# A recurrent-memory transformer block, forward and backward: two step loops whose x-attention was placed by a scheduler, written out engine by engine

## The chip, the cores and the metric

The kernel runs on one core of one Trainium2 chip. The metric is the device time of one execution in microseconds (us). Three executions of the kernel before took 8365.72, 8366.27 and 8371.87 us; the median is 8366.27 us.

## The reference

The input x has 2048 tokens of width 640. A layer norm gives xn. Branch A cuts xn into 64 segments of 32 tokens and carries a memory of 8 rows from one segment to the next, with 32 heads of 128 columns:

```
for s in range(64):
    h = concat([mem, xs])                     # 8 + 32 rows of 640
    q, k, v = h @ Wq, h @ Wk, h @ Wv          # each (32 heads, 40 rows, 128)
    scores = (q @ k.T) * scale
    scores = where(mask, scores, -1e9)        # memory rows see all 40, token rows look back
    o = (softmax(scores) @ v) @ Wo
    mem, out_s = o[:8], o[8:]                 # the new memory is the next step's input
```

Branch B is a gated feed-forward net (width 1728) on the same xn; the output is x + A(xn) * silu(B(xn)). The kernel also returns all gradients: of x, the first memory, Wq, Wk, Wv, Wo and the three matrices of B. Everything is bf16 with fp32 accumulation.

Only the eight memory rows make the 64 steps depend on each other. The 32 token rows of a segment need the memory as keys and values, but nothing waits for their outputs inside the loop.

## The kernel before

The work is done in phases, one after the other: layer norm and branch B forward; `phase3_Afwd`; `phase3b_out` (output projection); `phase4_Abwd`; `phase6_Awgrads` (weight gradients of A); `phase5_Bbwd_ln`.

`phase3_Afwd` first projects 672 tokens in one batch, and then runs the forward loop. `chain(t)` (L381) is the memory step: the projections of the new rows (L404, `packed_proj`, tile `pj`, 40 matmuls of 512 columns for each of v, k and q; 24 further tokens ride along in each step), the turned keys and queries (`packed_sel`), the scores of the memory rows (`psT`, L417), their softmax (L424 to L439), the product with v (`pom`, L448), the product with Wo (`packed_out`, L304, 64 matmuls of 320 columns), and `packed_fold` (L316), which turns the result into `hx`, the next step's input (L456).

The token rows are handled in tiles of three segments (`tl = t // 3`): 120 rows, in eight units of four heads. `kprep(tl, qd)` (L460) turns one unit's keys of the coming tile into `kT`; `xattn(tl, qd)` (L470) does one unit of the finished tile: load q and v, turn q (`qpt`), scores (`xsp`), maximum, exponentials on ACT (L501), normalising on POOL (`xP`, L506), turning (`xpp`, L510), product with v (`xpo`, L515), store. All turned tiles share one PSUM buffer (`tag="xt", bufs=1`), and most working tiles have one buffer.

The order on each engine is decided by the framework's scheduler: `chain(t)` is emitted under `tc.high_priority()` (L533), and the 16 units of a tile are emitted behind its three chain steps (L535). The first chain step of a tile reads all of the `kT` that eight `kprep` units have written.

`phase4_Abwd` is the same for the gradient, from the last step to the first: `chain(t)` (L639) with one projection (`packed_proj` of `gox`), `psd` (L682), the softmax gradient, `pgkv`, `pgq` (L721), three `packed_out` (L724) and `packed_fold` into `gox` (L729); `part1(tl, qd)` (L737) is a unit of the token rows. A tile's turned values are loaded at its first step as one tile `vTt` (L652), and the gradient rows go out to memory and come back in another layout (`gOst`, L670).

`phase6_Awgrads` (L835) goes over 8 groups of heads and, in each, 22 tiles: `t6` (L859) turns dS, three products `r6p` (L867), their turned copies `t6g` (L874), and 24 matmuls into the gradient of h (L882, L883).

SP (SyncE) issues most loads, POOL most stores, each in its own order; an issue that has to wait holds back those behind it.

Of the kernel before, what the change touches and what calls it, by code (L numbers as in the profile page):

```python
# [9 lines left out]
BF16 = mybir.dt.bfloat16  # L10
# [3 lines left out]
ALU = mybir.AluOpType  # L14
# [26 lines left out]
class K:  # L41
# [55 lines left out]
    def setup_consts(self):  # L97
# [17 lines left out]

        selb = const.tile([P, 2, 8], F32, name="selb")
        nc.gpsimd.memset(selb[:], 0.0)
        for a in range(2):
            nc.gpsimd.affine_select(out=selb[:], in_=selb[:], compare_op=ALU.not_equal, fill=1.0,
                                    base=-64 * a, pattern=[[-32, 2], [-1, 8]], channel_multiplier=1)  # L120
        self.selb = selb

    def build_masks(self, pool, scr):
# [21 lines left out]
        mcol = pool.tile([n, 3], F32, name="mcol")  # L145
        nc.vector.tensor_copy(mcol[:], a1[:, 0:nm].rearrange("p (s c) -> p s c", c=8)[:, :, 0])
# [10 lines left out]
        self.mask3, self.mask1, self.mcol = mask3, mask1, mcol  # L157

    def setup_dram(self):
# [18 lines left out]
        self.QS = mk("QS", (T, 32, HD))  # L178
        self.KS = mk("KS", (T, 32, HD))
        self.VS = mk("VS", (T, 32, HD))  # L180
        self.GOS = mk("GOS", (T, 32, HD))
        self.NB0 = 672
        self.QX0 = mk("QX0", (self.NB0, HD))
        self.KX0 = mk("KX0", (self.NB0, HD))
        self.VX0 = mk("VX0", (self.NB0, HD))
# [3 lines left out]
        self.PR, self.DSR, self.VTD = [], [], []  # L189
        for tl in range(self.NTL):  # L190
# [3 lines left out]
            self.VTD.append(mk(f"VTD{tl}", (P, H, n)))  # L194
        self.PM = mk("PM", (T, P, 240))
        self.GXP = mk("GXP", (T, P, 2, H, 8), F32)
# [13 lines left out]
    def x_src(self, tl, X0, XS, c0, c1):  # L210
        nx = self.geo(tl)[2]
        x0 = 96 * tl
        if x0 + nx <= self.NB0:
            return [(0, nx, X0[x0:x0 + nx, c0:c1])]
        t0 = (x0 - self.NB0) // 24
        if nx == 96:
            return [(0, 96, XS[t0:t0 + 4, 8:32, c0:c1])]
        return [(0, 24, XS[t0, 8:32, c0:c1]), (24, 32, XS[t0 + 1, 8:16, c0:c1])]
# [8 lines left out]
    def load_x(self, dst, off, srcs, eng):  # L227
        for (a, b, src) in srcs:
            eng.dma_start(dst[off + a:off + b, :], src)

    def load_m(self, dst, tl, XS, c0, c1, eng):
        ns, nm, nx, n = self.geo(tl)
        eng.dma_start(dst[0:nm, :], XS[3 * tl:3 * tl + ns, 0:8, c0:c1])
# [38 lines left out]
def packed_proj(k, ps, tag, x, W, st, cp):  # L272

    nc = k.nc
    for b in range(2):
        pj = ps.tile([P, 512], F32, name="pj", tag=tag)
        for dc in range(k.DC):
            for g in range(4):
                c0 = g * 1024 + b * 512
                nc.tensor.matmul(pj[32 * g:32 * g + 32, :], x[:, dc, :], W[:, dc, c0:c0 + 512],  # L280
                                 start=(dc == 0), stop=(dc == k.DC - 1), tile_position=(0, 32 * g),
                                 skip_group_check=True)
        k.copy(st[:, b * 512:(b + 1) * 512], pj[:], eng=cp[b])


def packed_sel(k, ps, tag, st):

    pk = ps.tile([P, 8, 4, 8], F32, name="psel", tag=tag)
    for j in range(8):
        k.nc.tensor.matmul(pk[:, j, :, :], st[:, j * P:(j + 1) * P], k.sel[:], start=True, stop=True)  # L290
    return pk


def packed_out(k, pm, srcs):

    nc = k.nc
    last = len(srcs) - 1
    for si, (x, W) in enumerate(srcs):
        for i in range(16):
            for a in range(2):  # L300
# [1065 lines left out]
```

## Time and profile before

| | |
|---|---|
| profiled execution, its own time | 8372.95 us |
| its span (first to last instruction) | 8371.2 us |
| TensorE matmul (PE) busy | 6051.0 us, 72% |
| TensorE weight load (PEld) busy | 3745.5 us, 45% |
| VectorE (DVE), ScalarE (ACT), GpSimd (POOL) busy | 29%, 20%, 14% |
| mean granted TensorE clock | 0.79 |

PE busy adds up the durations of matmuls that overlap in the pipeline, so it is no measure of how well the engine is used; the start of one matmul to the start of the next is. The granted clock is given as a share of 2.4 GHz: 1.0 is full speed, 0.5 is half (1.2 GHz). The rows that are used are in a section below.

### The profile page before, as it was taken

What the parts mean: (1) busy time and instruction counts of PE and PEld (TensorE: products, weight loads), DVE (VectorE), ACT (ScalarE), POOL (GpSimd) and SP (SyncE); (2) the same over time, 40 slices, a digit from 0 to 9 for tenths busy, and PEclk for the clock granted to TensorE, in tenths of its full rate; (3) what the DMA queues carried; (4) which work ended last, traced back from release to release, by engine and by line L of the source; (5) the groups of instructions that cost most, each with busy time, mean ns of one, the idle gap of its engine ahead of it and who ended that gap; (6) DMA issues with size and microseconds to landing.
All of it is one profiled execution on the core that took longest, in us unless ns stands there. A gap on an engine that the chain in (4) does not pass through costs nothing. (4 is left out here: it accounts for less than half of the span.)

```text
span 8371.2 us, 165393 instructions
## 1 busy us (share of the span) xinstructions
PE 6051.0 (72%) x67061; PEld 3745.5 (45%) x67142; DVE 2389.6 (29%) x7360; ACT 1672.1 (20%) x4414; POOL 1131.0 (14%) x1812
## 2 busy tenths in 40 slices
PE   7687666666666648576666777758888888787588
PEld 3354444444444435344444454545555555543234
DVE  5232222222222222233223233322222222202362
ACT  3232222222222221111111111111111111101111
POOL 0001111111111110233333333200000000000000
PEclk9796676666667769776666677789999999997699
DMA  5652222222222235433333344342222222246574
GB/s 186 219 172 66 77 78 75 75 71 76 74 77 74 82 95 155 144 108 107 107 105 111 106 119 122 100 98 72 71 70 71 71 74 78 74 104 170 175 193 103
DMA packets 858763, 880.27 MB, mean 105 GB/s; under 512 B 324472, under 2 KB 751944, under 8 KB 848272
## 3 DMA queue, kind: packets, MB, share of 16 engines
q1 hardware_dynamic: 507863, 542.29, 22.7%
q10 hardware_dynamic: 296440, 232.27, 9.5%
q0 software_dynamic: 53696, 95.13, 4.5%
q8 instruction: 529, 8.67, 0.5%
q14 instruction: 235, 1.92, 0.1%
HBM read 558.97 MB, written 310.36 MB: 104 GB/s over the span
## 5 line engine op out<-in xcount | busy, mean ns | idle before, releaser
L882 PE MATMUL g<-w,gT 128*96 128x512 bf16 (+1 forms) x2112 | 640.8, 401 | 0.0
L899 PE MATMUL wg<-gr,hr 120*128 120x512 bf16 (+1 forms) x2640 | 582.0, 379 | 5.2 <-DVE ghacc L888 3.6
L782 POOL DMA_DIRECT2D GXP<-gks x512 | 382.9, 861 | 711.8 <-DVE gks L90 637.4
L883 PE MATMUL g<-w,gT 128*96 128x128 bf16 (+1 forms) x2112 | 477.9, 226 | 0.0
L899 PEld LDWEIGHTS <-hr 120*128 120x128 bf16 (+1 forms) x2640 | 252.7, 98 | 322.8 <-issue 28.6
L92 ACT CAST gr<-r6p 120x512 bf16<-120x512 f32 (+1 forms) x352 | 205.8, 585 | 915.6 <-PE r6p L867 810.5
L510 PE MATMUL xpp<-ident,xP 120*120 120x120 bf16 (+1 forms) x704 | 109.3, 297 | 378.2 <-POOL xP L506 378.2
L882 PEld LDWEIGHTS <-gT 128*96 128x96 bf16 (+1 forms) x2112 | 271.6, 129 | 206.9 <-issue 41.7
L501 ACT ACTIVATE xE<-xsp,xnm 120x120 bf16<-120x120 f32 (+1 forms) x704 | 243.1, 356 | 380.9 <-DVE xnm L497 343.9
L304 PEld LDWEIGHTS <-gkv 128*8 128x8 bf16 x8192 | 226.2, 105 | 200.7 <-DVE gkv L715 39.0
L280 PEld LDWEIGHTS <-hx 128*32 128x32 bf16 x7680 | 206.8, 100 | 224.6 <-issue 49.3
L304 PE MATMUL gpm<-WvT,gkv 128*8 128x320 bf16 x4096 | 263.5, 444 | 32.8 <-DVE gkv L715 32.8
L506 POOL TENSOR_TENSOR xP<-xE,xrz 120x480 bf16<-120x480 bf16 (+1 forms) x176 | 168.9, 960 | 768.0 <-issue 428.9
L883 PEld LDWEIGHTS <-gT 128*96 128x96 bf16 (+1 forms) x2112 | 272.4, 129 | 0.0
L892 POOL CAST gxo<-ghacc 96x640 bf16<-96x640 f32 (+1 forms) x22 | 15.8, 716 | 1881.9 <-DVE ghacc L889 1842.6
L510 PEld LDWEIGHTS <-xP 120*120 120x120 bf16 (+1 forms) x704 | 77.0, 189 | 405.8 <-POOL xP L506 398.7
L304 PE MATMUL pm<-Wo,oTm 128*8 128x320 bf16 x4032 | 248.0, 430 | 4.2 <-DVE oTm L450 1.8
L682 PE MATMUL psd<-gmT,vTt 128*120 128x8 bf16 (+1 forms) x2048 | 150.8, 210 | 133.4 <-DMA vTt<-VTD 130.4
L888 DVE TENSOR_TENSOR ghacc<-ghacc,g 96x512 f32<-96x512 f32 (+1 forms) x154 | 105.2, 683 | 485.4 <-PE g L882 485.4
L515 PE MATMUL xpo<-vr,xPT 120*120 120x128 bf16 (+1 forms) x704 | 107.9, 293 | 162.2 <-DMA vr<-VS 77.5
L767 DVE CUSTOM_DVE_ANT_0 gprx<-gdp,gPx 96x120 f32<-96x120 f32 (+1 forms) x704 | 158.1, 270 | 233.8 <-PE gdp L762 209.2
L90 DVE CAST stg<-pj 128x512 bf16<-128x512 f32 x192 | 132.8, 692 | 314.5 <-PE pj L280 314.3
(298 smaller groups left out, 12032.5 us busy)
## 6 DMA issues: line engine op xcount, KB each, us to landing
OR<-xos POOLq DMA_DIRECT2D x168, 120.0 KB, 2.5
VTD<-gvT POOLq DMA_DIRECT2D x168, 120.0 KB, 3.6
vTt<-VTD SPq DMA_DIRECT2D x21, 960.0 KB
orr<-OR SPq DMA_DIRECT2D x8, 2520.0 KB
PR<-xP POOLq DMA_DIRECT2D x168, 112.5 KB, 3.4
dS<-DSR ACTq DMA_DIRECT2D x158, 112.5 KB
P<-PR SPq DMA_DIRECT2D x158, 112.5 KB
hb_tok<-HB ACTq DMA_DIRECT2D x40, 432.0 KB
```

What stands on the lines that cost most here:

```text
L92: return nc.scalar.copy(out, in_)
L280: nc.tensor.matmul(pj[32 * g:32 * g + 32, :], x[:, dc, :], W[:, dc, c0:c0 + 512], start=(dc == 0), stop=(dc == k.DC - 1), tile_position=(0 ...
L304: nc.tensor.matmul(pm[p0:p0 + 8, 0:320], x[:, h, :], W[:, h, 320 * b:320 * b + 320], start=(si == 0 and i == 0), stop=(si == last and i == ...
L501: nc.scalar.activation(E[0:n, j, :], sp[:, j, :], ACT.Exp, bias=nmx[0:n, j:j + 1], scale=k.scale, accum_out=Z[0:n, j:j + 1])
L506: nc.gpsimd.tensor_tensor(Pb[0:n], E[0:n], bc_last(rz[0:n], n), ALU.mult)
L510: nc.tensor.transpose(pp[:, j, :], Pb[0:n, j, :], k.ident[0:n, 0:n])
L682: nc.tensor.matmul(psd[:, h, :], vT[:, h, :], gmT[:, h, :], start=True, stop=True)
L767: nc.vector.tensor_tensor_reduce(pr[0:nx, j, :], dp[:, j, :], Px[0:nx, j, :], -k.scale, 0.0, ALU.mult, ALU.add, Dx[0:nx, j:j + 1])
L782: nc.gpsimd.dma_start(k.GXP[3 * tl + s, :, :, h0:h0 + 4, :], ks[:, s])
L882: nc.tensor.matmul(g5[0:nx, :], gT[:, i, j, 0:nx], Ws[i][:, j, 0:512], start=f, stop=l)
L883: nc.tensor.matmul(g1[0:nx, :], gT[:, i, j, 0:nx], Ws[i][:, j, 512:640], start=f, stop=l)
L899: nc.tensor.matmul(accs[dc][:], hr[0:n, tl, dc * P:(dc + 1) * P], grs[tl][0:n, i, :], start=(tl == 0), stop=(tl == NTL - 1))
```

## The change

Both loops are written in a fixed order. `in_order` ties each instruction of a loop to the one written before it on the same engine, so that the scheduler moves nothing. The x-attention unit is cut into stages (`turn_q`, `scores`, `soft`, `norm`, `turn_p`, `pv`; backward `turn`, `dprob`, `dsoft`, `gmem`), with loads of their own (`ld`, `ld_k`), and a table says which stage of which unit stands in which gap of the memory step (W0 to W2 between the projections, G1 to G6 between the later stages). Each step takes at most three units, but for the first backward step, which takes eleven; `pv` and the third `turn_p` of a unit come in the next step. In some gaps stand matmuls whose result nobody reads (`WARM`: 15 in a forward step, 10 in a backward step). The memory chain uses three fixed PSUM banks; the units rotate through five.

Other parts of the change: the memory rows look at their own segment's 40 rows rather than at the tile's 120; `vt`, `vTt` and `krow` hold one step rather than three; the fold sums its halves on ACT and DVE and turns a bf16 tile; `gOst` is turned on PE and no longer goes through memory; q and v share one DRAM tensor. In `phase6_Awgrads` the three products come in another order. Weight tiles of 96 or 120 columns are padded with zeros to 128.

```diff
+def in_order(k, start):
...
+    for ins in tc.nc.cur_bb.bb.instructions[start:]:
+        p = last.get(ins.engine)
+        if p is not None:
+            tc.add_manual_dep(ins, p.name, mybir.DependencyInfo(mybir.DependencyClass.NoSync, mybir.DependencyReason.DATA),
+                              reason="written order")
+        last[ins.engine] = ins
...
+def fold_add(k, pm, pool):
...
+    for c in (0, 160):
+        up = pool.tile([64, 160], F32, name="fup", tag="fup")
+        nc.scalar.copy(up[:], pm[64:128, c:c + 160])
+        nc.vector.tensor_tensor(fs[:, c:c + 160], pm[0:64, c:c + 160], up[:], ALU.add)
...
+            WARM = dict(G1=1, G2=2, G3=3, G4=4, G5=3, G6=2)
...
+                sk = stage()
+                half(Wk_, 0, sk, 'v')
+                half(Wk_, 1, sk, 'v')
+                gap("W0")
...
+                half(Wq, 1, sq, 'v')
+                gap("W1")
...
+                gap("W2")
+                psT = bview(bC, 40, 2, 8, 16)
+                for h in range(H):
+                    nc.tensor.matmul(psT[:, h // 16, :, h % 16], kT[:, h, 40 * s:40 * s + 40], qmT[:, h, :], start=True, stop=True)
...
+                gap("G1")
+                ps2 = bview(bC, P, 2, 40, bf=True)
...
+                gap("G2")
+                ps3 = bview(bC, 40, 2, P, bf=True)
...
+                gap("G3")
+                pom = bview(bC, P, H, 8)
...
+                gap("G4")
+                packed_out(k, pm, oTm, Wo, True, True)
+                fs = fold_add(k, pm, ch)
+                gap("G5")
+                pt = fold_turn(k, bC, fs)
...
+                gap("G6")
...
+                    for i in range(WARM.get(g, 0)):
+                        nc.tensor.matmul(bB[:], k.ident[:], Wq[:, 0, 0:512], start=True, stop=True)
...
+                if g == "W0":
+                    at(pv, t - 1, 0)
+                    at(turn_p, t - 1, 2)
...
+                elif g == "W1":
+                    at(pv, t - 1, 1)
+                elif g == "W2":
+                    at(pv, t - 1, 2)
...
+                elif g == "G1":
+                    at(scores, t, 0)
+                    at(turn_q, t, 2)
...
+                elif g == "G2":
+                    at(scores, t, 1)
+                    at(scores, t, 2)
+                    for u in kb[0:2]:
+                        kprep(*u)
...
+                elif g == "G3":
+                    at(soft, t, 0)
+                    at(soft, t, 1)
+                elif g == "G4":
+                    at(soft, t, 2)
+                    for i in range(3):
+                        at(norm, t, i)
+                elif g == "G5":
+                    at(turn_p, t, 0)
+                    at(turn_q, t + 1, 0)
...
+                elif g == "G6":
+                    at(turn_p, t, 1)
+                    at(turn_q, t + 1, 1)
+                    for u in kb[2:]:
+                        kprep(*u)
...
+            WARM = dict(G1=2, G2=3, G5=3, G6=2)
...
+                for a in range(2):
+                    nc.tensor.transpose(pgo[:, a, :], gmT[:, a].rearrange("p q h -> p (q h)"), k.ident[:])
+                nc.scalar.copy(gOst[:], pgo[:])
...
+                    if t == T - 1:
+                        if g == "G6":
+                            for u in batch[t]:
+                                ld_next()
+                                for f in (turn, dprob, dsoft, gmem):
+                                    f(*u)
...
+                    elif g == "W0":
+                        at(turn, t, 0)
+                    elif g == "W1":
+                        at(turn, t, 1)
+                        if t + 1 < T - 1:
+                            at(gmem_ld, t + 1, 2)
+                    elif g == "G1":
+                        at(dprob, t, 0)
+                    elif g == "G2":
+                        at(dsoft, t, 0)
+                    elif g == "G3":
+                        at(turn, t, 2)
+                        at(dprob, t, 1)
+                    elif g == "G4":
+                        at(dsoft, t, 1)
+                        at(gmem_ld, t, 0)
+                    elif g == "G5":
+                        at(dprob, t, 2)
+                        at(gmem_ld, t, 1)
...
-                for i, (lh, rh) in enumerate(((dST, kr), (dS, qr), (Pr, gor))):
+                for i, (lh, rh) in enumerate(((Pr, gor), (dS, qr), (dST, kr))):
```

On ACT in the forward loop, the stretch before the first step of a new tile read like this in the kernel before (`xE` are one unit's four exponentials, `qT` the copy of its turned queries, `xos` the copy of its result, `stg` a projection, `sTm` the memory scores):

```order
L92 CAST stg<-pj 128x512 x3
L92 CAST xos<-xpo 120x512
L486 COPY qT<-qpt 128x480
L501 ACTIVATE xE,xZ<-xsp,xnm 120x120 x4
L92 COPY kT_5752<-kpt 128x4x96
L486 COPY qT<-qpt 128x480
L501 ACTIVATE xE,xZ<-xsp,xnm 120x120 x4
L92 CAST xos<-xpo 120x512
...
L421 ACTIVATE sTm<-psT,mcol 120x256
```

One step of the changed kernel on ACT, from its `PTm` on (`xP` are now the exponentials, `fup` the fold, `xv` the result, `Em` the memory softmax):

```order
L604 ACTIVATE xP_5748,xZ<-xsp,xnm 120x120 x4
L604 ACTIVATE xP_5749,xZ<-xsp,xnm 120x120 x4
L604 ACTIVATE xP_5750,xZ<-xsp,xnm 120x120 x4
L348 COPY fup<-bank_5764 64x160 x2
L574 COPY xqT_5746<-qpt 128x4x120
L574 COPY xqT_5747<-qpt 128x4x120
L557 COPY kT_5741<-kpt 128x12x32
L634 CAST xv<-xpo 120x512 x2
L92 CAST stg<-bank_5764 128x512
L92 CAST stg<-bank_5765 128x512
L634 CAST xv<-xpo 120x512
L491 CAST sTm<-bank_5766 40x256
```

The exponentials of three units now stand together behind one another, and their results' copies stand in the next step; before, a unit's copies and exponentials alternated, one unit behind the other, between the projections and `sTm`.

On SP in the backward loop, the kernel before issued in this order around a tile's first step (`vTt` is the tile's 128x3840 load, `gOst` the gradient rows that come back, `gqx`, `gvr`, `gor`, `gPx` the loads of a unit):

```order
L668 DMA GOS<-gstg 4x32x1024
L652 DMA vTt<-VTD 128x3840
L670 DMA gOst<-GOS 128x1x128 x2
L229 DMA gqx<-QS 96x1x512
L233 DMA gvr<-VS 24x1x512
L229 DMA gvr<-VS 96x1x512
L229 DMA gor<-GOS 96x1x512
L663 DMA xp<-GXP 128x512
```

In the changed kernel (`gqv` is q and v of a unit together, `vTt` one step's 128x1280):

```order
L848 DMA xp<-GXP 128x8x64
L888 DMA GOS<-gstg 4x32x1024
L963 DMA gqv<-QVS 24x2x512
L246 DMA gqv<-QVS 96x2x512
L246 DMA gor_40752<-GOS 96x1x512
L970 DMA gPr<-PR 120x480
L832 DMA vTt<-VTD 128x1280
L834 DMA gPm<-PM 128x80
L837 DMA Qst<-QVS 128x1x128 x2
L842 DMA krow<-KS 8x4096
```

The `vTt` that is issued here belongs to the step after the one whose gradient rows `GOS` stores; before, it belonged to the same step and the `psd` of that step waited for it. `gOst` has left the queue.

## Rows read from the trace of the kernel before

**Rows 1.** Windows of four stretches: us, busy time by engine, granted clock, DMA share, GB/s.

```profile
core 0: us, PE busy (x) PEld busy (x) DVE busy (x) ACT busy (x) POOL busy (x), PEclk, DMA share, GB/s
599.00:2936.00 2337.00, 1578.11 (x21112) 988.20 (x21112) 605.11 (x1550) 613.88 (x2138) 392.02 (x587) 0.69 0.26 75
2936.00:3085.00 149.00, 50.33 (x415) 34.16 (x415) 31.77 (x96) 42.12 (x196) 36.29 (x59) 0.50 0.27 74
3421.00:5457.00 2036.00, 1395.10 (x24223) 957.38 (x24224) 626.46 (x3161) 314.26 (x779) 672.33 (x1107) 0.71 0.40 108
5540.00:7400.00 1860.00, 1554.46 (x11662) 949.84 (x11660) 474.25 (x1091) 300.33 (x588) 15.76 (x22) 0.97 0.24 71
```

**Rows 2.** Timeline of DVE, forward loop: start us, us; the end of three steps.

```profile
1442.07 0.20 DVE L456 CAST hx<-pfold 128x40 bf16<-128x40 f32 x1 [0.90 <-PE pfold L316]
1506.68 0.20 DVE L456 CAST hx<-pfold 128x40 bf16<-128x40 f32 x1 [1.15 <-PE pfold L316]
1530.76 0.20 DVE L456 CAST hx<-pfold 128x40 bf16<-128x40 f32 x1 [0.97 <-PE pfold L316]
```

**Rows 3.** Timeline inside the long step: one x-attention unit, and the next one's start.

```profile
1468.98 0.66 PE L492 MATMUL xsp<-kT,qT 128*120 128x120 bf16 x4 [0.70 <-ACT qT L486]
...
1472.54 0.98 POOL L506 TENSOR_TENSOR xP<-xE,xrz 120x480 bf16<-120x480 bf16 x1 [3.38 <-issue]
...
1477.45 0.66 PE L492 MATMUL xsp<-kT,qT 128*120 128x120 bf16 x4 [0.70 <-ACT qT L486]
```

**Rows 4.** Waits of PE, 1200 to 2600 us: total us, times, longest.

```profile
PE xpp L510 <- POOL xP L506: 186.5, 75, 4.2
```

**Rows 5.** Windows: a short step, part of a long one, two `packed_out` (columns as Rows 1).

```profile
1418.00:1442.00 24.00, 19.90 (x309) 12.30 (x306) 7.33 (x18) 6.37 (x20) 3.20 (x5) 0.79 0.32 91
...
1457.00:1504.00 47.00, 22.40 (x209) 15.58 (x213) 9.73 (x27) 12.46 (x50) 9.82 (x14) 0.50 0.25 73
1411.80:1415.90 4.10, 4.10 (x64) 2.04 (x64) 0.41 (x1) 0.00 (x0) 0.08 (x1) 0.54 0.29 95
4125.90:4130.40 4.50, 4.50 (x136) 2.87 (x128) 0.00 (x0) 0.00 (x0) 0.00 (x0) 1.00 0.20 62
```

**Rows 6.** Timeline of PE: one group of each kind at the full clock.

```profile
1410.28 0.99 PE L448 MATMUL pom<-PTm,vt 120*128 120x8 bf16 x32 [0.46 <-ACT PTm L445]
...
1418.25 2.34 PE L280 MATMUL pj<-Wv,hx 128*32 128x512 bf16 x40
...
1452.61 0.43 PE L515 MATMUL xpo<-vr,xPT 120*120 120x128 bf16 x4
...
1453.05 0.38 PE L490 MATMUL xsp<-mask,ident 120*120 120x480 bf16 x1
...
4125.96 2.34 PE L304 MATMUL gpm<-WkT,gkv 128*8 128x320 bf16 x64
```

**Rows 7.** Waits of PE, 3500 to 4800 us, backward loop.

```profile
PE gvpt L751 <- DMA gvr<-VS: 133.2, 49, 6.5
PE psd L682 <- DMA vTt<-VTD: 91.0, 14, 7.9
```

**Rows 8.** Timeline of PE in the weight gradients: one tile of 176.

```profile
6101.18 0.38 PE L859 MATMUL t<-ident,dS 120*120 120x120 bf16 x4
6102.58 0.43 PE L867 MATMUL r6p<-r,dST 120*120 120x128 bf16 x4 [1.02 <-DVE dST L861]
6103.69 0.38 PE L867 MATMUL r6p<-r,P 120*120 120x128 bf16 x4 [0.67 <-ACT gr L92]
...
6105.26 0.38 PE L882 MATMUL g<-w,gT 128*96 128x512 bf16 x1
6105.48 0.22 PE L883 MATMUL g<-w,gT 128*96 128x128 bf16 x1
6105.53 0.38 PE L882 MATMUL g<-w,gT 128*96 128x512 bf16 x1
...
6108.25 0.38 PE L859 MATMUL t<-ident,dS 120*120 120x120 bf16 x4
```

**Rows 9.** Groups by line: weight loads of 96 and of 128 columns, busy and mean ns.

```profile
L882 PEld LDWEIGHTS <-gT 128*96 128x96 bf16 (+1 forms) x2112 | 271.6, 129 | 206.9 <-issue 41.7
L899 PEld LDWEIGHTS <-hr 120*128 120x128 bf16 (+1 forms) x2640 | 252.7, 98 | 322.8 <-issue 28.6
```

More of the change, by code (lines that the diff above doesn't have):

```diff
@@ L114, in setup_consts @@
         self.sel = sel
[L116 to L121, printed above, removed]
+        with tc.tile_pool(name="mkscr", bufs=1) as scr:
+            self.build_masks(const, scr)
     def build_masks(self, pool, scr):
@@ L286, in packed_sel @@
[L286 to L300, printed above, removed]
-                for b in range(2):
-                    h = 16 * a + i
-                    p0 = 32 * (2 * a + b)
-                    nc.tensor.matmul(pm[p0:p0 + 8, 0:320], x[:, h, :], W[:, h, 320 * b:320 * b + 320],
-                                     start=(si == 0 and i == 0), stop=(si == last and i == 15),
-                                     tile_position=(0, p0), skip_group_check=True)
@@ new lines, in packed_sel, with packed_out @@
+def packed_sel(k, pk, st, b):
+    for j in range(4 * b, 4 * b + 4):
+        k.nc.tensor.matmul(pk[:, j, :, :], st[:, j * P:(j + 1) * P], k.sel[:], start=True, stop=True)
+def packed_out(k, pm, x, W, first, last):
+    nq = x.shape[2]
+    for i in range(16):
+        for a in range(2):
+            for b in range(2):
+                h = 16 * a + i
+                p0 = 32 * (2 * a + b)
+                k.nc.tensor.matmul(pm[p0:p0 + nq, 0:320], x[:, h, :], W[:, h, 320 * b:320 * b + 320],
+                                   start=(first and i == 0), stop=(last and i == 15),
+                                   tile_position=(0, p0), skip_group_check=True)
@@ L471, in xattn, with turn_q, scores @@
+            def turn_q(tl, qd):
+                n = k.geo(tl)[3]
+                r = uu.pop(("q", tl, qd))
+                pt = ps.tile([P, 4, n], BF16, name="qpt", tag="x", bufs=5)
+                for j in range(4):
+                    nc.tensor.transpose(pt[:, j, :], r[0:n, j * P:(j + 1) * P], k.ident[0:n, 0:n])
+                qT = qTs[qd % 2]
+                nc.scalar.copy(qT[:, :, 0:n], pt[:])
+            def scores(tl, qd):
                 ns, nm, nx, n = k.geo(tl)
-                c0 = qd * 512
@@ new lines, in chain @@
+                dS = ch.tile([P, 2, 40], BF16, name="dSm", tag="dSm", bufs=2)
+                nc.vector.tensor_tensor(dS[:], u[:], Pm[:], ALU.mult)
+                bdS = ch.tile([P, 2, 16, 8], BF16, name="bdS", tag="bdS")
+                bd(nc.vector, bdS, dS)
+                if 0 < t < T - 1:
+                    loads(t - 1)
+                gap("G2")
+                packed_out(k, pm, gvT, WvT, True, False)
+                ps3 = bview(bC, 40, 2, P, bf=True)
+                for a in range(2):
+                    nc.tensor.transpose(ps3[:, a, :], dS[:, a, :], k.ident[:])
@@ L799, in mem_rows @@
+            loads(T - 1)
+            load_k(T - 1)
+            load_xp(T - 1)
+            ride(T - 1)
+            for t in range(T - 1, -1, -1):
+                chain(t, gap_of(t))
+            in_order(k, start)
 def mem_rows(k, srcs):
```

860 lines of the change are left out of this document (508 added, 352 removed).

## The prediction

> **What bounds the kernel now.** I read the windows by phase first, then the timeline around the end of each step, then PE's waits, then the granted clock.
>
> The two loops hold more than half of the span: 2337 us for the 64 forward steps and 149 us for the units left behind them, 2036 us for the 64 backward steps [rows 1]. The weight gradients of A take 1860 us. The other phases keep their instructions, and I count them as unchanged.
>
> A forward step takes 36.5 us on average (2337 / 64), but no step takes that: the ends of three steps stand 64.6 and 24.1 us apart [rows 2]. Two of three steps take about 24 us, the third about 64. The third is the one in which a tile's remaining x-attention units have to be done, because the next step's scores read keys that the scheduler has put behind them. There the units run one behind the other: the scores of one unit and those of the next stand 8.47 us apart, and the pair of rows between shows where the time goes, from the scores over ACT's exponentials to 0.98 us on POOL, and back [rows 3]. PE's largest wait in the forward loop is this one, 186.5 us for POOL's product in 1400 us [rows 4]. So the long step is a chain of latencies with an idle PE, not a lack of PE time.
>
> An idle PE also loses its clock. The stretch of such units was granted 0.50, a short step 0.79; the same 64 matmuls took 4.10 us at 0.54 and 2.34 us at 1.00 [rows 5, 6].
>
> The backward loop is bounded by loads: `psd` waits up to 7.9 us for the tile's values, 14 times, and a unit's first turn up to 6.5 us for its rows, 49 times [rows 7]. With units of the token rows ordered between the chain's stages, each such wait stands in the memory chain.
>
> **Forward loop.** The change spreads eight units over three steps and lets a unit's stages stand in different gaps, so the 8.47 us of one unit run beside the memory chain. What is left is PE's own work per step, since the gaps are now full. By the rows at the full clock [rows 6]:
> - six half projections, 120 matmuls of which 40 take 2.34 us: 7.0
> - some 90 small ones (16 `packed_sel`, 32 + 32 for scores and `pom`, transposes, fold) at 0.99 / 32 = 0.031 each: 2.8. The scores had 120 weight columns and now have 40; I take the rate of `pom`, and at half that rate it would be 1.0 more
> - `packed_out`: 2.34
> - units: 8/3 per step, each a masked product of 0.38 and five groups of four at up to 0.43 (the score group is split in two): 2.5 each, 6.7; `kprep` another 8/3 groups: 1.1
> - 15 unread matmuls of 512 columns. In the weight gradients one of 512 and one of 128 columns follow every 0.27 us (6105.26 to 6105.53), so 512 columns take 0.22 [rows 8]: 3.3
>
> Sum 23.2 us. Waits that no fill covers: after the fold's four short ACT and DVE operations, and at `hx`. I add 1.0 and take 24.2 us. DVE and ACT had 605 and 614 us of work in the 64 steps and little more behind them, some 10 us a step [rows 1], so they can delay a stage but do not set the rate.
>
> The loop then takes three light steps without units (20 us each), 61 steps of 24.2, some 10 us for the eight first `kprep` that stand ahead of it, and five groups of left-over units at the end. Thirteen units are left; at 8.47 us each in series they would be 110 us, in groups of two or three about 12 us a group, 60 us. Sum 60 + 1476 + 10 + 60 = 1606 us against 2337 + 149: **880 us less**.
>
> **Backward loop.** The step's loads are issued in the step before, and the gradient rows are turned on PE (two transposes and a copy) where they went to memory and back. So the waits of rows 7 should go. PE per step, same rates: one projection 2.34; some 90 small ones 2.7; three `packed_out` 7.0; 8/3 units of six groups at 0.43, 6.9; 10 unread matmuls 2.2. Sum 21.1 us. The softmax gradient, four short DVE operations in series, has 0.65 us of unread matmuls beside it; and ACT copies two units' turns ahead of the memory scores. I add 1.2 and take 22.3 us against 31.8 (2036 / 64).
>
> Ahead of that stand eight short units (40 rows, about 4 us each) and the first step, which does eleven units one behind the other. A unit's serial path (two turns, a product, eight DVE operations, a last product) has no POOL operation in it; I take 5.8 us, two thirds of the forward unit's 8.47 [rows 3], and half of 8.47 for a short one. With 8.47 for the eleven it would be 29 us more. Sum 32 + 22 + 64 + 63 x 22.3 = 1523 us against 2036: **513 us less**.
>
> What would be late next: SP has to issue some 25 DMAs per backward step; the `xp` load is the last of a step and is used some 7 us into the next, which is the tightest of them. The DMA engines were 0.40 busy; the same bytes in the shorter step make 0.57 (0.40 x 31.8 / 22.3) [rows 1], which still leaves room.
>
> **Weight gradients of A.** A tile takes 7.07 us, 1.02 of it in PE's wait for the turned dS and 0.67 in the wait for ACT's copy [rows 8]. With the two products that don't need the turn first, both waits have something beside them. The gain lies between nothing, if DVE's additions of the tile before hold the turn as they do now, and 1.69 us. I take half, 0.85 us for each of 176 tiles: **150 us less**.
>
> The padding to 128 columns I count at nothing. A weight load of 96 columns takes 129 ns, one of 128 columns 98 [rows 9]; but the pair of matmuls follows every 0.27 us, which is 640 columns at the full clock, so the loads lie beside the matmuls [rows 8].
> The Trainium skill (TensorE: Matmul & The Clock Gate, section Weight-path perf modes) says that a fast weight load is used when a load has the full 128 columns, and the shorter row agrees. If loads set the pace there, 4224 loads would give back 31 ns each, 131 us more; the spacing in the row says they do not.
>
> **Sum.** 880 + 513 + 150 = 1543 us less. The profiled execution took 8372.95 us by its own count, 7 us above the median of the three runs; 8373 - 1543 = 6830, and **6825 us** against the median.
>
> **The rivals.**
> - *The clock falls in the gaps all the same.* Many fills are transposes and small products. The short step of today holds PE busy for 19.9 of 24 us and is still granted 0.79 [rows 5], so about 10 us run at half, which loses 5 us of full-speed work. The same loss in 124 steps is 620 us: 7445 us. For it: the stretch of units, all transposes and small products, was granted 0.50. Against it: there PE mostly waited, and the unread matmuls stand in most of the long gaps.
> The Trainium skill (same page, section PE-mode transpose) says that transposes do not count as PE activity in the way that matmuls do; by that rule this rival is the likelier one, at the same 7445 us, and the 0.50 of rows 5 agrees without proving it.
> - *The backward loop stays bound by loads.* SP's order is now fixed, and one load that waits for its buffer holds the rest. If the step stays at 31.8 us, 513 us are not gained: 7340 us. For it: rows 7 are such waits. Against it: the loads now have a step of lead.
> - *The units' latency stays.* If a stage in a gap waits for POOL as today, three units a step still cost most of 8.47 us each, and only the tail, the backward loop and the weight gradients gain: about 7700 us. Against it: scores and results of a unit now lie a step apart.
> - *Slower.* In the written order nothing can pass a stage that waits. If each step meets two late loads of today's longest kind, 7.9 + 6.5 = 14.4 us, the 124 steps lose 1786 us against the forecast: 8610 us. From 1543 / 124 = 12.4 us of such waits per step on, the kernel is slower than before. For it: the loads still share one SP queue; against it: the waits of rows 7 came in one or two of three steps, with loads issued in the step that used them.
>
> **How the numbers follow.** Forecast 0.62, the clock 0.20, the loads 0.08, the latency 0.05, slower 0.05. The forecast's own range is 6480 to 7150: at the low end the added waits (1.0 and 1.2 us a step) and all of the 1.69 us are gone, 285 us, with a little off the groups that I took at 0.43; at the high end 2.6 us more per step. The range reaches over the clock and the loads: 6480 to 7450. A difference of 0.2% is about what a measurement of this kernel can tell; the chance of faster is 0.94, within 0.2% 0.01, slower 0.05.
>
> **What the profile of the changed kernel would show.** Right: ends of forward steps evenly 23 to 25 us apart with no third long step, backward 21 to 24; a granted clock of 0.95 or more in both loops; PE's waits for POOL's product and for `vTt` and unit loads near nothing; the weight gradients near 1710 us. Wrong: a clock near 0.8 in the loops (the first rival), PE waiting for DMA in the backward loop (the second), or `xpp` waiting for POOL (the third). A stage in the table whose wait is longer than the fills ahead of it would show as one idle of the same length in every step.

## The result and the profile after

The changed kernel takes **6966.84 us** (median, 6958.37 to 6975.43) against 8369.07 of the kernel before in the same comparison: a ratio of 0.8323, 95% interval 0.8308 to 0.8337. The forecast was 6825 us, the range 6480 to 7450. The profiled execution spans 6956.7 us, 1414.5 us less than before. By the first TensorE instruction of each stage in the two traces (the forward row begins with the batch projection):

| Stage | Change forecast, us | Change measured, us |
|---|---|---|
| forward loop and the units behind it | -880 | -762 |
| backward loop | -513 | -457 |
| weight gradients of A | -150 | -201 |
| all else | 0 | +5 |

Windows of the kernel after: the forward loop, the units left behind it, two parts of the backward loop, the weight gradients. They answer to [rows 1]. The columns are the busy time (and count) of each engine, the granted clock, the DMA share and GB/s.

```profile
core 0: us, PE busy (x) PEld busy (x) DVE busy (x) ACT busy (x) POOL busy (x), PEclk, DMA share, GB/s
611.00:2241.00 1630.00, 1459.64 (x22457) 773.83 (x22456) 709.72 (x2112) 630.91 (x2222) 588.90 (x792) 0.87 0.40 103
2241.00:2326.00 85.00, 31.18 (x339) 20.63 (x339) 19.96 (x62) 33.89 (x155) 39.04 (x49) 0.54 0.54 150
2801.00:3700.00 899.00, 747.93 (x14513) 461.47 (x14515) 358.25 (x1704) 228.00 (x747) 296.98 (x517) 0.86 0.56 144
3700.00:4240.00 540.00, 478.89 (x9659) 298.33 (x9650) 223.54 (x1024) 141.83 (x459) 180.71 (x311) 0.92 0.56 144
4451.00:5982.00 1531.00, 1389.52 (x10683) 787.78 (x10682) 381.07 (x845) 363.21 (x668) 15.84 (x22) 0.98 0.30 79
```

The loops are granted 0.86 to 0.92, more than the 0.69 and 0.71 of before and less than I expected. The ends of the steps, by line of the kernel after (count, duration, first and last start):

```profile
L536 DVE CAST hx<-bank x63: 199/200/200, 639.0 to 2223.1; 128x40 bf16<-128x40 f32 x63
...
L947 DVE CAST gox<-gbank x64: 199/200/201, 2718.0 to 4240.2; 128x40 bf16<-128x40 f32 x64
```

62 forward intervals in 1584.1 us are 25.55 us each. They lie between 23.7 and 27.9: the long third step of [rows 2] is gone. Of the backward intervals the first takes 82.9 us, the other 62 take 23.21 on average: 24.3 in the first half of the loop, 21.3 in the last third, with single steps between 19.3 and 29.7.

What is left of waits in 1100 us of the forward loop (engine, line, what it waited for: us, times, longest):

```profile
ACT stg L92 <- DMA KS<-stg: 193.4, 39, 6.1
DVE vt L484 <- ACT stg L92: 180.5, 43, 5.4
...
PE bank L662 <- ACT stg L92: 92.0, 43, 3.2
...
PE xpp L623 <- POOL xP L615: 0.6, 1, 0.6
```

The wait for POOL's product [rows 4] fell from 186.5 us in 75 waits, in 1400 us, to 0.6 us in one wait, in these 1100. In its place stands a wait that nobody had in view. The timeline of one step shows it (start, duration, then in brackets the idle time before and its releaser; rows of POOL, ACT, DVE and PE):

```profile
1460.52 0.76 POOL L456 DMA_DIRECT2D KS<-stg  x1
...
1467.41 1.07 ACT L92 CAST stg<-bank 128x512 bf16<-128x512 f32 x2 [4.74 <-DMA KS<-stg]
...
1468.03 2.35 DVE L484 COPY vt<-stg 8x512 bf16<-8x512 bf16 x8 [4.02 <-ACT stg L92]
1470.31 0.22 DVE L499 TENSOR_REDUCE mmx<-bank 128x2 f32<-128x80 bf16 x1
...
1466.05 0.37 PE L572 MATMUL qpt<-ident,xq 120*128 120x120 bf16 x4
1468.53 0.38 PE L662 MATMUL bank<-Wq,ident 128*128 128x512 bf16 x1 [2.11 <-ACT stg L92]
```

A step has three stage tiles (keys, queries, values), and the ring of `stg` (the set of buffers that these tiles take in turn) has two buffers, where the kernel before had three. The change made other rings shorter too: `gstg` and `gks` in the backward loop have one buffer each, where the kernel before had two. The value tile reuses the key tile's buffer, which is still being stored to `KS`: the store is issued at 1460.52 behind a store of the x-attention and lands almost 7 us later. ACT's copy of the values waits for it, PE's next unread matmul waits for ACT since it writes the same bank, and DVE's eight copies come late and delay the maximum of the softmax. The granted clock is 0.5 from 1469.25 to 1472.66; it falls soon after PE's 2.11 us of idle time.

The backward loop, 800 us of it, which answers to [rows 7]:

```profile
ACT gks L1027 <- DMA GXP<-gks: 112.6, 47, 9.0
DVE gkv L871 <- DMA xp<-GXP: 106.3, 21, 7.4
...
PE gbank L1096 <- DVE gkv L871: 59.3, 33, 5.6
...
PE gbank L326 <- ACT gstg L92: 36.4, 9, 5.6
...
PE gbank L892 <- DMA gPr<-PR: 4.8, 6, 0.9
```

PE's wait for `vTt` is gone, and of its waits for loads of the units 5.6 us are left (4.8 for `gPr`, 0.8 for `gor`). Late are now the `xp` load, and the store of a unit's products, whose one buffer `gks` holds ACT.

### The profile page after: what moved, and what is told of

Read it like the earlier page. It is cut to its first block, busy times and chain, and to the rows that moved or that the text cites. A ratio compares the mean times of both kernels' runs of the same rounds, so it can differ in the third digit from the quotient of the medians.

```text
span 6956.7 us, 170429 instructions
## 1 busy us (share of the span) xinstructions
PE 5767.0 (83%) x69516; PEld 3253.2 (47%) x69516; DVE 2419.9 (35%) x7541; ACT 1878.1 (27%) x5180; POOL 1184.8 (17%) x1811
## 5 line engine op out<-in xcount | busy, mean ns | idle before, releaser
L1199 PE MATMUL g<-w,gT 128*128 128x512 bf16 x2112 | 622.7, 385 | 0.8 <-ACT gT L92 0.8
L1200 PE MATMUL g<-w,gT 128*128 128x128 bf16 x2112 | 466.9, 221 | 0.0
L662 PE MATMUL bank<-Wq,ident 128*128 128x512 bf16 x960 | 352.1, 474 | 138.1 <-ACT stg L92 138.1
L1199 PEld LDWEIGHTS <-gT 128*128 128x128 bf16 x2112 | 209.3, 99 | 220.9 <-issue 13.9
L1096 PE MATMUL gbank<-WqT,ident 128*128 128x512 bf16 x640 | 226.7, 461 | 83.6 <-DVE gkv L871 83.6
L92 ACT COPY gT<-t6g 128x480 bf16<-128x480 bf16 (+1 forms) x352 | 191.8, 545 | 331.1 <-PE t6g L1190 215.8
L604 ACT ACTIVATE xP<-xsp,xnm 120x120 bf16<-120x120 f32 (+1 forms) x704 | 239.7, 359 | 28.9 <-DVE xrz L614 18.2
L1241 PE MATMUL oa<-gow,orr 120*128 120x512 bf16 x704 | 197.2, 383 | 35.3 <-DMA orr<-OR 35.3
L1190 PE MATMUL t6g<-ident,gr 120*128 120x120 bf16 (+1 forms) x2112 | 187.9, 219 | 43.3 <-ACT gT L92 40.8
L1200 PEld LDWEIGHTS <-gT 128*128 128x128 bf16 x2112 | 209.0, 99 | 0.3
L337 PE MATMUL gbank<-WvT,gkv 128*8 128x320 bf16 x4096 | 202.1, 366 | 0.0
```

What stands on the lines that cost most here:

```text
L92: return nc.scalar.copy(out, in_)
L337: k.nc.tensor.matmul(pm[p0:p0 + nq, 0:320], x[:, h, :], W[:, h, 320 * b:320 * b + 320], start=(first and i == 0), stop=(last and i == 15), ...
L604: nc.scalar.activation(Pb[0:n, j, 0:n], sp[0:n, j, :], ACT.Exp, bias=nmx[0:n, j:j + 1], scale=k.scale, accum_out=Z[0:n, j:j + 1])
L662: nc.tensor.matmul(bB[:], k.ident[:], Wq[:, 0, 0:512], start=True, stop=True)
L1096: nc.tensor.matmul((bA if g[0] == "W" or g == "G1" else bB)[:], k.ident[:], WqT[:, 0, 0:512], start=True, stop=True)
L1190: nc.tensor.transpose(pt[:, j, :], gr[0:n, i, j * P:(j + 1) * P], k.ident[0:n, 0:n])
```

## The experiments

Two theories. **T1:** the loops would run at the pace of PE's work; the 142 us above the forecast are waits for buffers and loads that a fixed order cannot pass, and the half clock behind them. **T2:** the clock falls because the fills are transposes and small products, whatever the waits. Times are medians; ratios are to the kernel before. In stages with the same code the profiles differ by up to 12 us in one stage (weight gradients) and some 20 us in all, so I read each edit in its own stage.

**The store of KS issued earlier, from ACT's queue.**

```diff
                 half(Wk_, 1, sk, 'v')
+                dump(sk, k.KS[t], nc.scalar)
                 gap("W0")
...
-                dump(sk, k.KS[t])
```

> The store of the memory's key rows (KS) is issued from ScalarE's queue right behind the second key half instead of from GpSimd behind an x-attention store, so the two-buffer stage ring should be free when the value half is copied. Theory 1 (the loops run at the pace of PE's own work, and the missing 142 us are waits that the fixed order cannot pass, plus half clock behind them): ScalarE's wait for KS, 193 us in 1100 us of the forward loop, goes; the forward step falls from 25.55 us to 22 to 23.5 and the clock of the loop rises from 0.87 to 0.93 or more; 6967 - 62 x 2.5 = 6810, between 6770 and 6850. Theory 2 (the clock falls because the fills are transposes and small products): the direct wait on PE goes, 92 us in 1100 us, part of it refilled; the clock stays at 0.85 to 0.89, 6880 to 6920. Theory 3 (the wait moves to the next late buffer): 6950 to 6980.

Measured: 6924.68 us, 0.8279 (0.8262 to 0.8295), in none of the three ranges. The forward step is 25.42 us, only 0.13 less; 20 us of the gain lie in stages that the edit does not touch. T1's number failed. The trace says why (timeline, then ACT's waits):

```profile
1449.95 0.52 ACTq L456 DMA_DIRECT2D KS<-stg  x1
...
1459.82 1.07 ACT L92 CAST stg<-bank 128x512 bf16<-128x512 f32 x2 [6.46 <-DMA KS<-stg]
...
ACT stg L92 <- DMA KS<-stg: 127.5, 26, 7.2
...
ACT stg L92 <- DMA QVS<-stg: 55.3, 10, 7.6
```

In this step the store was issued 9.9 us ahead of the copy, and the copy still waits for it. That step is a long one: over all steps the edit moved the issue only 1.0 us forward (a median of 4.1 us after `hx` is ready, against 5.2), and from the issue to the copy pass 7.5 us, against 7.1. The queries' store, in the other buffer, begins to hold the copy too: the two rows add up to 182.8 us, against 193.4 for `KS` before. So the edit hardly did what it was meant to do, and it did not decide between the theories.

**Three buffers in the stage ring.** The room comes from small tiles of the memory chain that share a buffer.

```diff
-                    return ch.tile([P, 1024], BF16, name="stg", tag="stg", bufs=2)
+                    return ch.tile([P, 1024], BF16, name="stg", tag="stg", bufs=3)
...
-                oTm = ch.tile([P, H, 8], BF16, name="oTm", tag="oTm")
+                oTm = ch.tile([P, H, 8], BF16, name="oTm", tag="qmT")
```

> Three buffers in the forward loop's stage ring in place of two (the room comes from small tiles of the memory chain that now share one buffer); KS is stored as in the changed kernel. Theory 1 (this ring is the miss of the forward loop): ScalarE's wait for KS (193 us in 1100 us) and the wait of G1's first unread matmul behind it (92 us, 43 times) are gone; the step falls by those 2.1 us to 23.0 to 23.6, 6967 - 63 x 2.1 = 6835, between 6800 and 6860. Rival (the store's landing only covers another link of the same chain, as the earlier store suggested, whose step fell by 0.13 us with a third of the wait gone): 6930 to 6960, with another wait of 60 us or more in front of G1.

Measured: **6728.56 us**, 0.8034 (0.8019 to 0.805), 238 us less than the changed kernel, where T1 expected 107 to 167. The step falls to 21.64 us. The window of the loop, and PE's three largest waits in 1100 us:

```profile
637.00:1979.00 1342.00, 1287.11 (x21935) 711.18 (x21935) 705.99 (x2065) 640.68 (x2199) 580.77 (x782) 0.98 0.47 122
...
PE qpt L578 <- DMA xq<-QVS: 24.8, 24, 2.5
PE kpt L561 <- DMA kr<-KS: 10.9, 13, 1.6
PE bank L520 <- DVE Pm L515: 5.2, 14, 0.6
```

The wait for `KS` is gone, PE is busy 96% of the time, and the granted clock is 0.98 with the same transposes and small products. T2 falls for the forward loop; the backward loop, with its 0.84 to 0.90 in this run, was not put to that test. The gain of 3.9 us a step is larger than the 2.1 us that PE waited directly. The median starts of the chain's stages, counted from `hx`, show where the rest comes from. Up to the scores the two kernels are alike (9.9 us). The turn of the scores starts 2.3 us earlier with three buffers, the turn of the softmax 3.3 earlier, since DVE's late copies no longer hold the maximum, and the product with Wo 4.1 earlier, at a clock that is no longer halved behind the wait.
The Trainium skill (TensorE: Matmul & The Clock Gate, section PE-mode transpose) says that transposes do not count as PE activity in the way that matmuls do. This trace does not bear it out as the cause in the forward loop: 0.87 and 0.98 were granted to the same transposes.

**No unread matmuls.**

```diff
-            WARM = dict(G1=1, G2=2, G3=3, G4=4, G5=3, G6=2)
+            WARM = {}
...
-            WARM = dict(G1=2, G2=3, G5=3, G6=2)
+            WARM = {}
```

> The 1600 unread matmuls of the two loops are left out; nothing that is computed changes. They take 352 and 227 us of PE, 9 us a step. If they are only cost (PE sets the pace and the clock does not depend on them): up to 350 us less, 6600 to 6700. If they only fill time in which PE would wait anyway and hold the clock: the forward loop's granted clock falls from 0.87 to 0.7 or below, and the time rises by 50 to 300 us, 7020 to 7270. If neither matters: 6930 to 7000.

Measured: 6898.26 us, 0.8246 (0.8231 to 0.826). None of the three cases came: the clock fell, and yet it was 69 us faster. The forward step is 25.06 us; the backward loop did not move (23.25 against 23.21). Forward window and PE's largest wait:

```profile
639.00:2192.00 1553.00, 1222.62 (x20998) 714.55 (x20995) 695.56 (x2065) 618.44 (x2199) 582.52 (x782) 0.82 0.41 106
...
PE bank L497 <- ACT sTm L491: 115.8, 44, 4.1
```

They took 352 us of PE in the forward loop and cost about 33 us there (the next stage starts at 2293.3 instead of 2326.0). The two profiled executions differ by 51 us; the other 19 of these lie behind the forward loop, where every stage differs by less than 10. Nearly all of the unread matmuls stand where PE would wait anyway: without them the product with Wo starts 2.0 us earlier in the step, but its 64 matmuls take 3.8 us instead of 2.5, at the lower clock. So the forward sum, which counted 3.3 us a step for them as part of the pace, named the wrong bound.

**The order left to the scheduler, in both loops.**

```diff
-            in_order(k, start)
```

> Same program text as the changed kernel, but the order of each engine in both loops is left to the scheduler (the two calls that fix the written order are left out); static banks, stage splitting and the order of the weight gradients stay. If the gain is in where the program places the stages, which the scheduler mostly keeps: 6900 to 7100. If it is in fixing the order: the scheduler pulls fills together and pushes them out again, long steps come back, and most of the 1218 us of the two loops are lost: 7700 to 8200.

Measured: 6975.64 us, 0.8338 (0.832 to 0.8356): no difference to the changed kernel that can be told. The written order itself, which is the head of the change, is worth next to nothing in sum; the gain must lie in the other parts. By stages the fixed order gains 58 us up to the end of the forward tail (step 25.55 against 26.70) and loses 32 us in the backward loop (23.21 against 23.02, and a shorter first step of 68.2 under the scheduler).

**Whole units in one gap, in fixed order, and the same with the forward order left to the scheduler.**

```diff
+            def whole(tl, qd):
+                for f in (turn_q, scores, soft, norm, turn_p, pv):
+                    f(tl, qd)
...
+                elif g == "G1":
+                    at(whole, t, 0)
...
+                elif g == "G3":
+                    at(whole, t, 1)
...
+                elif g == "G5":
+                    at(whole, t, 2)
```

> Forward loop with whole units: all six stages of a unit stand in one gap (G1, G3, G5), one unit behind the other, in written order; all else as in the changed kernel. If splitting the stages over the gaps is what shortened the step: each of 8/3 units a step adds its latency, 8.47 us, less the 2.5 of PE that it has anyway, 16 us a step: about 41 us a step and 6967 + 1000 = 7970, between 7600 and 8100. If static banks and the fixed order are what did it: 6960 to 7100.

> The same whole units, and in the forward loop alone the order of each engine is left to the scheduler. If the stages' place in the program is the gain and the scheduler can't find it: forward steps of 33 to 38 us on average, uneven in threes as before the change: 7450 to 7800. If the scheduler finds the overlap by itself once the banks are static: about the 26.7 us of the staged program under the scheduler, 6980 to 7100.

The units' loads move to other gaps with them. Measured: 8172.19 us, 0.9756 (0.9742 to 0.9771), somewhat above the expected range, and 7172.79 us, 0.8563 (0.8546 to 0.8579), in neither of the two ranges. In fixed order the step is 44.63 us, near the 41 worked out from a unit's latency. PE's wait in 1000 us, and two units of the timeline:

```profile
PE xpp L623 <- POOL xP L615: 245.5, 59, 5.0
...
1116.28 0.58 PE L623 MATMUL xpp<-ident,xP 120*128 120x120 bf16 x4 [4.57 <-POOL xP L615]
...
1126.42 0.58 PE L623 MATMUL xpp<-ident,xP 120*128 120x120 bf16 x4 [4.01 <-POOL xP L615]
...
1132.42 3.90 PE L337 MATMUL bank<-Wo,oTm 128*8 128x320 bf16 x64
```

This is [rows 3 to 5] again: POOL's product late in every unit, and the 64 matmuls at half clock (3.90 us). So in a fixed order the split of the stages over the gaps is worth 1205 us. With the scheduler it is worth 172 us in the forward stage; the rest of the 197 us between the two runs (7173 against 6976) lies mostly in the backward loop, whose order is fixed in one and free in the other. Given the same units, evenly spread and on static banks, the scheduler finds most of the overlap, 28.76 us a step where the kernel before took 36.5, and no step is longer than 31.9 us. Its wait for POOL's product in 1100 us:

```profile
PE xpp L623 <- POOL xP L615: 53.0, 88, 1.8
```

My expectation for this run was wrong. Which of the even spread, the static banks and the other parts of the change (the memory rows' 40 columns, the shorter fold, the loads) does that was not tried.

**The xp load earlier; then two gks buffers as well.**

```diff
                 if t > 0:
+                    if t < T - 1:
+                        load_xp(t - 1)
                     load_k(t - 1)
...
-                ks = fl.tile([P, ns, 2, 4, 8], F32, name="gks", tag="gks", bufs=1)
+                ks = fl.tile([P, ns, 2, 4, 8], F32, name="gks", tag="gks", bufs=2)
```

> In the backward loop the load of xp is issued as soon as its last reader is done, ahead of the key rows and of two units' loads, some 8 us earlier on SyncE's queue. Theory 1: the wait of gkv for xp (106 us in 800 us, 21 times, up to 7.4 us) goes, and PE's wait behind it (59 us in 800 us); the steps of the first half of the loop fall from 24 to 26 us to 21 to 22.5; 6967 minus 60 to 110: 6855 to 6905. Rival (the DMA engines are the bound there, 0.56 busy in that stretch, so another load becomes late in its place, the key rows or a unit's rows): 6940 to 6980, with a new DMA wait of 50 us or more in the same 800 us.

> As the early xp load, and two buffers for gks, the products of a unit's memory rows that wait for the store of the unit before (152 us of ScalarE's waits in 750 us with the early load, up to 12.3 us). If these waits stand in the chain (ScalarE's next copies, gstg above all, queue behind gks): the backward step falls from 22.7 to 21.8 or less, 6902 minus 40 to 70: 6830 to 6865. If ScalarE has room for them: 6890 to 6910.

Measured: 6902.44 us, 0.8249 (0.8232 to 0.8267), step 22.71; and 6852.85 us, 0.8174 (0.8155 to 0.8193), step 21.99. The second edit finds the room for its buffer in small tiles of the chain that share one. With the load alone, ACT's wait for the store grew in its place, and PE's largest wait is now the one for `gstg`, ACT's copy of a projection, which stands behind it on ACT (800 us of the loop):

```profile
ACT gks L1029 <- DMA GXP<-gks: 169.3, 46, 12.3
...
PE gbank L326 <- ACT gstg L92: 47.9, 15, 6.1
```

The early load alone took PE's wait for `gkv` from 55.2 to 13.2 us in 750. The second buffer took away both rows shown. By the medians the early load gave 64 us and the second buffer 50 more; in the backward stage itself, by the profiles, it was 31 and 53. The wait for the store had grown from 112.6 to 169.3 us once the load was in time, so it took back a part of the first edit until it was mended too.

**The weight gradients: order of the products, and padding.**

```diff
-                for i, (lh, rh) in enumerate(((Pr, gor), (dS, qr), (dST, kr))):
+                for i, (lh, rh) in enumerate(((dST, kr), (dS, qr), (Pr, gor))):
```

> Changed kernel, with the three products of the weight gradients' tile back in the order of before (the product that needs the turned dS first). If the order is what took 201 us off that phase: the tile goes back from 5.8 to 6.6 to 7.1 us and the time to 7110 to 7180. If the padding to 128 columns did it: 6950 to 6985.

Measured: 7255.67 us, 0.865 (0.8635 to 0.8664), 289 us more than the changed kernel and more than I expected. The median distance of tiles, by DVE's additions into the gradient of h, goes from 5.86 to 7.28 us. The groups of the turned product in 1100 us of that phase (busy us, mean ns, then idle time before and its releasers), after and with the old order:

```profile
L1179 PE MATMUL r6p<-r,dST 120*128 120x128 bf16 x456 | 45.1, 222 | 35.7 <-ACT gr L1182 34.2 <-DVE dST L1173 1.5
```

```profile
L1179 PE MATMUL r6p<-r,dST 120*128 120x128 bf16 (+1 forms) x382 | 38.5, 224 | 101.0 <-DVE dST L1173 86.6 <-DVE wgo L90 13.4 <-DMA r<-GOS 1.0
```

PE's wait for the turned dS ahead of this product goes from 1.5 to 86.6 us. The timeline of one tile, after and with the old order:

```profile
4745.24 0.38 PE L1172 MATMUL t<-ident,dS 120*128 120x120 bf16 x4
...
4746.68 0.38 PE L1199 MATMUL g<-w,gT 128*128 128x512 bf16 x1
4746.90 0.39 PE L1179 MATMUL r6p<-r,dST 120*128 120x128 bf16 x4
4747.12 0.22 PE L1200 MATMUL g<-w,gT 128*128 128x128 bf16 x1
```

```profile
5200.61 0.38 PE L1172 MATMUL t<-ident,dS 120*128 120x120 bf16 x4
5202.02 0.40 PE L1179 MATMUL r6p<-r,dST 120*128 120x128 bf16 x4 [1.03 <-DVE dST L1173]
```

With the new order matmuls into the gradient of h (L1199, L1200) stand between the turn and the turned product; with the old order nothing does, and the wait of [rows 8] is back. The order is the whole gain of this phase. With the old order the tile is even slower than the 7.07 us of [rows 8]; the other edits there cost something under that order, which was not taken apart.

```diff
-                        nc.tensor.matmul(g5[:], gT[:, i, j, :], W[:, j, 0:512], start=f, stop=l)
+                        nc.tensor.matmul(g5[0:n, :], gT[:, i, j, 0:n], W[:, j, 0:512], start=f, stop=l)
```

> Changed kernel, with the weight loads of the two g products of that phase back to the 96, 120 or 40 columns that the tile has. If loads lie beside the matmuls, as I counted: 6955 to 6985. If a narrow load's extra 31 ns are on the path of each of 4224 loads: 6967 + 131 = 7100.

Measured: 6982.96 us, 0.8326 (0.8309 to 0.8344); a tile every 5.88 us against 5.86. The loads without and with padding:

```profile
L1199 PEld LDWEIGHTS <-gT 128*120 128x120 bf16 x1352 | 180.2, 133 | 98.6 <-issue 4.7 <-ACT gT L92 0.2
```

```profile
L1199 PEld LDWEIGHTS <-gT 128*128 128x128 bf16 x1368 | 135.4, 99 | 140.4 <-issue 8.1 <-ACT gT L92 0.2
```

A load of 120 columns takes 34 ns longer, and PEld had idle time for it. Only the loads of these two products were tried; the forecast counted the same ones.

**All that helped, with and without the unread matmuls.** Three stage buffers, early `xp`, two `gks` buffers, and `gride` loaded a step ahead (the gradient rows that ride along in the projection; a new tile of them is needed every fourth step).

```diff
                         at(dsoft, t, 2)
-                        if t > 0:
-                            load_xp(t - 1)
+                        if t > 9 and (t - 9) % 4 == 0:
+                            ride_ld((t - 9) // 4 - 1)
```

> Three stage buffers in the forward loop, early xp load and two gks buffers in the backward loop, and gride (needed every fourth step) loaded one step before its use. The stages lie apart in time, so the gains should add: 6967 - 238 (stage ring) - 114 (xp and gks) - 20 to 40 for gride (PE waited 19.5 us for it in 750 us, 8 times): 6575 to 6615. If the shorter backward step meets other late loads (gqv, 30 us in 750): 6620 to 6660.

> The same without the 1600 unread matmuls. With three stage buffers PE is 96% busy in the forward loop at a clock of 0.98, so it should now set the pace: 15 unread matmuls of 0.215 us are 3.2 us of a step. If they are only cost: forward step 21.6 to 18.5 us, and 1 to 2 us off the backward step: 340 to 400 us less than with them, about 6200 to 6280. If the clock needs them (it fell from 0.87 to 0.82 without them when the ring was short): the forward step gains 0.5 to 1.5 us as the cut then did, 6480 to 6580. If the chain of latencies sets the pace right below PE's: within 30 us of the run with them.

Measured: **6633.26 us**, 0.7913 (0.79 to 0.7927), and 6627.55 us, 0.7909 (0.7895 to 0.7922), without them. That is 18 us above the range for gains that add, and in the second range, the one with `gqv` as the next late load: the backward step is 21.67, and PE waits 45.6 us in 800 for it. By the profiles the gains do add: the ring gave 246 us in the forward stage and the two backward edits 84 in theirs, 330 in sum, and this profiled execution is 334 us shorter than the changed kernel's (231 in the one stage and, with `gride`, 100 in the other). The sum in the expectation took 114 for the backward edits, from the medians. Forward windows with, then without:

```profile
640.00:1980.00 1340.00, 1277.48 (x21717) 704.49 (x21710) 701.23 (x2052) 636.58 (x2181) 575.79 (x776) 0.98 0.48 122
```

```profile
640.00:1970.00 1330.00, 1161.85 (x20591) 681.39 (x20583) 695.04 (x2028) 628.50 (x2166) 569.28 (x768) 0.89 0.48 122
```

The same step (21.83 and 21.92 us) at 95% and at 87% of PE, at 0.98 and at 0.89. The unread matmuls buy clock and cost time, and the two cancel: without them the product with Wo starts 1.1 us earlier in the step (15.5 us after `hx` against 16.6, medians), and its 64 matmuls take 3.7 us instead of 2.1. So a PE that is 95% busy is no proof that PE's sum sets the pace here. What does is probably the chain of one step, but no run shows that. T1 is right about the waits; PE as the bound under them was not borne out.

## Why the prediction was right, and where it was not

- **The long third step goes.** Right. Whole units in a fixed order bring back POOL's wait and the half clock, so the latency of a unit was read rightly. But the remedy was credited to the wrong part. Under the scheduler even whole units, on the new banks and evenly spread, have no long step. Of the 762 us of the forward stage, that run already has 532; the split of the stages adds 172 under the scheduler, and the written order the last 58. In the backward loop the written order costs 32. That the scheduler put the units behind one another of itself, as the prediction says, is not shown: the one buffer for all turned tiles in the kernel before is a rival that was not tried by itself.
- **A forward step of 24.2 us.** Measured 25.55. The term that failed is "Waits that no fill covers", taken at 1.0 us: the ring of two stage buffers was in the code, and I did not price the wait for the store in it. Three buffers take 3.9 us off the step, to 21.6, so the sum of 23.2 was too high by itself (PE was busy 20.8 us a step then, 1287.11 / 62). Two errors met half-way, and that 24.2 came near 25.55 is in part luck. That PE's sum is the pace was not borne out: 3.3 us of it were unread matmuls that can go for nothing.
- **A clock of 0.95 or more in both loops.** Wrong: 0.87, and 0.86 to 0.92. The first rival had the sign. In the forward loop it had not the reason: the clock followed the wait, not the kind of fill. Nor did it have the price there, since the time it lost came back with three buffers. The backward loop still has 0.87 and 0.94 in the run with all that helped, and why was not settled.
- **60 us of left-over units.** 85 us, at a clock of 0.54. With the step this makes most of the 118 us that the forward term missed.
- **A backward step of 22.3 us.** 23.21 on average. The term that failed is the same one, added waits of 1.2 us: the `xp` load was named as the tightest and was late, but it was not priced; the one buffer of `gks` was not named. Without these two waits the step is 21.99. The start of the loop was sized well: 42 us for the short units against 32, and 82.9 for the eleven units with one step against 86.
- **The loads of rows 7 stop bounding the backward loop.** Right; neither of those waits is in the list after.
- **Weight gradients 150 us less.** 201 less: 1.21 of the 1.69 us went, where I took half. The order does it. What stands beside the wait is more than the two other products that were argued: matmuls into the gradient of h stand there too.
- **Padding at nothing.** Right for the loads that were counted: 16 us, inside the scatter, and a tile's distance the same within 0.02 us.

The measured time lies 142 us above the forecast: the forward and backward terms missed 118 and 56 us, and the weight gradients gave 51 more than forecast, which took part of that back. What sets the 21.7 us that both loops now reach was not settled; the forward loop's PE waits are small there and spread over many lines.

## What to carry to other kernels

Before crediting a fixed order, take it away again with all else in place: here that cost nothing that can be told, and most of the forward gain came even with whole units under the scheduler. When an order is fixed by hand, list for every ring of buffers what the reuse waits for, stores included: a store's landing counts from its issue, and one ring that the change had made one buffer shorter cost 238 us here, nearly twice what the direct wait on PE showed (2.1 us a step, some 130 us). Before taking a busy engine's sum as the pace, take out the work on it that nobody reads: if the step does not move, the sum was not the bound. And when one late buffer is mended, look whether the next one's wait has grown before judging the edit.

## What the runs showed of the hardware

A store of the stage tile's keys (256 KB) took 6.3 to 8.3 us from issue to landing on POOL's queue in the changed kernel, all 64 of them together:

```profile
DMA to landing us min/median/max: 6.3/6.9/8.3
```

For ACT's queue the trace has no landing times. From the issue there to the copy that reuses the buffer passed a median of 7.5 us, against 7.1 from POOL's.

Fifteen unread matmuls a step lifted the granted clock of the forward loop from 0.82 to 0.87 with two stage buffers and from 0.89 to 0.98 with three. The time did not follow: the step is 0.5 us longer with them in the first pair and 0.1 shorter in the second.
